# Linear attention into a gated feed-forward layer, in fp32 split into two parts on one core: matmuls with a lower part last within each word of matmuls, and a new order of all words

## The chip, the core and the metric

The kernel runs on one core of a Trainium2 chip. The core has TensorE (PE: matmuls, and PEld: the loads of their stationary tiles), VectorE (DVE), ScalarE (ACT), GpSimd (POOL) and SyncE (SP, which issues the DMAs here). Each engine executes its own list of instructions in order and waits on semaphores for the others. The metric is the device time of one execution in microseconds (us).

## The reference

Attention with a decaying state over 32 batch-head pairs, 768 time steps and 48 columns, followed by a gated feed-forward layer over 3072 tokens:

```python
# q, k, v, alpha: (4, 8, 768, 48); w_gate, w_val: (384, 1536); w_out: (1536, 384)
for t in range(S):
    state = alpha[:, :, t, :, None] * state + einsum('bhd,bhe->bhde', k[:, :, t], v[:, :, t])
    y[:, :, t] = einsum('bhd,bhde->bhe', q[:, :, t], state)
x = y.transpose(0, 2, 1, 3).reshape(3072, 384)
g = x @ w_gate
silu = g * (1.0 / (1.0 + exp(-g)))
out = (silu * (x @ w_val)) @ w_out
```

The inputs of attention are float32; the three weight matrices arrive as float64, are read as pairs of 32-bit words and are cut to two float32 parts on the chip.

## The kernel before

**Precision.** Each operand of the large products is split into an upper part and a lower part, the rest that the upper part leaves (both in the format fp32r). A product of two operands is then three matmuls that add into the same PSUM tile: upper by upper, upper by lower, lower by upper. The fourth, lower by lower, is left out.

**Tiling.** The feed-forward layer takes 8 blocks of 384 tokens, and 12 slices of 128 of the hidden width for each, which are 96 steps (s = 0 to 95). Blocks 0 and 1 are each done in two parts (slices 0 to 6 of both, then 7 to 11 of both), with the partial sums of the output stored and read back between; the other blocks go one after the other. Attention is cut into 16 units of 192 time steps, in three chunks of 64; two units give the tokens of a block, so attention of later units runs between the products of earlier blocks.

**One step of the feed-forward layer** is made of these words:
- `g` and `v` (TensorE, `product`, L716): nine matmuls each into one PSUM tile (`gps` or `vps`, one buffer each): for each of three k-tiles (`kt`) the three matmuls above. The stationary operand is a weight tile (128x128), the moving one 128x384 of the turned x (`xT`).
- `sl` (ScalarE, L724): silu of g. `h` (VectorE, L728): its product with v. `hh` (ScalarE, L732): the upper part of h, `hl` (VectorE or GpSimd, L737): the lower part. h, hh and hl have two buffers each.
- `o` (TensorE, `out_product`, L748): nine matmuls, three for each of three PSUM tiles `ops0` to `ops2` (128 tokens each). The stationary operand is a tile of hh or hl, the moving one the upper or lower part of w_out. The sums stay in the ops tiles over the 12 steps of a block; `first` starts them and `last` closes them, and `ot` and `os` (or `pl`, the partial sums read back) take them out.

**One unit of attention** is made of loads (`La`, `Lk`, `Lq`, `V`), copies and transpositions into the layout of the scans (L397, L405 and L417), two scans of the decay over time (`G`, L461, and `f`, L470), products of k and q with their results (`mk`, L818 and L821; `q`), k turned back (`K`, L511, with its copies `kc` L515 and L516; or `kr`, L527, on VectorE), scores `S` (L552) and their mask `ma` (L586), the sums of k and v that are carried between chunks `B` or `Bw` (L576) with `ad` (L599 to L608) and `de`, a copy `vc` of V (`U`, L498), outputs `Y` (L630 to L647), their upper and lower parts `yh` and `yl` (L661, L665), and the repacking into x by DMA (`xr`, L701) or, for the first units, by TensorE (`R`, L687). Words `w0v0` to `w19p` cut the weights (L160 on ScalarE is one of their steps), and `wr`, `wc`, `Lc` and `ck` read inputs again to see whether they lie in the range that this path is made for; only if not, another path runs behind it.

**The order.** Nothing is scheduled by the compiler: the table `ORDER` is a list of words, each `engine:name@banks` with t for TensorE, v VectorE, s ScalarE, g GpSimd and y SyncE. A loop (L898 to L902) calls them in that order, and so fixes what each engine executes after what, which engine does a word that more than one can do, and which PSUM bank a tile takes (L895).

```python
BANKS = ("A0", "A1", "A2", "ops0", "ops1", "vps", "gps", "ops2")
...
for word in ORDER.split():
    e, name = word.split(":")
    name, *banks = name.split("@")
    todo.pop(name)(engines[e], *(BANKS[int(x)] for x in "".join(banks)))
```

## Time and profile before

| what | us |
|---|---|
| three runs | 552.26, 555.14, 554.64 |
| their median | 554.64 |
| the profiled execution, its own time | 552.74 |
| its span, from first to last instruction | 551.0 |

The profile is of one execution. A group in it is a set of instructions of one line, engine, operation and kind of tile: their count, busy time in us, the mean ns of one, and then the idle time of the engine just ahead of them with what ended it. TensorE's matmuls are pipelined, so one lasts longer (336 ns) than the time from one start to the next. In the chain of work that ended last a row is a start, a time and the work, with matmuls that follow each other closely in one row. A row of the stages has the stretch, its length, the busy time of TensorE's matmuls, of its weight loads, of VectorE, ScalarE and GpSimd with their counts of instructions, then the granted clock of TensorE, the share of the DMA engines and the GB/s that they moved. The chain of waits names for each group of an engine what released it: total us, count, longest.

### The profile page before, as it was taken

To read this page: it belongs to the slowest core of one execution; us is meant where nothing else is said; L and a number is where in the kernel's file an instruction comes from. 1 tells how busy PE (TensorE), PEld (TensorE's weight loads), DVE (VectorE), ACT (ScalarE), POOL (GpSimd) and SP (SyncE) were. 2 spreads that over 40 slices of the span, in tenths; PEclk is the share of its full clock that TensorE was granted. 3 is DMA by queue.
4 is the path that set the end of the run, shared out by engine and by line. 5 is a ranking of instruction groups with operands and counts; after the bars stand their busy time and mean duration, and the time that the engine had idled before them with its cause. 6 is when DMAs were issued, how large, how long until landed. Compare 5 with 4: busy or idle time off the path is not lost.

```text
span 551.0 us, 13702 instructions
## 1 busy us (share of the span) xinstructions
PE 536.4 (97%) x5510; PEld 523.7 (95%) x5510; DVE 384.8 (70%) x612; ACT 258.7 (47%) x581; POOL 136.5 (25%) x146
## 2 busy tenths in 40 slices
PE   4999999999999999999999999999999999999996
PEld 3899999999999989999999999999999999999996
DVE  7999999999999996766788378878765232321223
ACT  6998655353422232243332434235343345447775
POOL 7522124354314240122220322231230101001100
PEclk9999999999999999999999999999999999999999
DMA  8789859435668555343536526535351112334463
GB/s 254 193 246 292 249 145 251 130 95 133 164 170 223 134 130 152 82 119 79 119 100 184 158 56 178 135 87 165 82 159 47 47 49 82 104 106 131 123 181 100
DMA packets 95362, 77.61 MB, mean 141 GB/s; under 512 B 32832, under 2 KB 92224, under 8 KB 95296
## 3 DMA queue, kind: packets, MB, share of 16 engines
q1 hardware_dynamic: 94864, 76.12, 51.2%
q8 instruction: 44, 0.72, 0.6%
q10 hardware_dynamic: 432, 0.59, 0.3%
q14 instruction: 22, 0.18, 0.1%
HBM read 62.52 MB, written 5.90 MB: 124 GB/s over the span
## 4 chain that ended last, share of the span: by engine, by line
PE 90%; DVE 3%; SPq 2%; ACT 2%; DMA 1%; issue 1%; DVEq 0%; ACTq 0%
PE g L716 26%; PE v L716 26%; PE ops L748 26%; PE A L576 3%; PE y L647 2%; PE s L552 2%; PE y L630 1%; SPq L701 1%; PE y L631 1%; DVE AT L470 1%; PE pt L417 1%; PE kps L511 1%; DMA Le<-in_alpha_dram 1%; DMA L<-in_k_dram 1%; DVE Gs L461 1%
## 5 line engine op out<-in xcount | busy, mean ns | idle before, releaser
L716 PE MATMUL g<-xT,w 128*128 128x384 f32 x864 | 167.5, 337 | 1.0 <-issue 1.0
L716 PE MATMUL v<-xT,w 128*128 128x384 f32 x864 | 166.9, 337 | 0.3 <-DVE h L728 0.3
L748 PE MATMUL ops<-w,hh 128*128 128x384 f32 x576 | 157.4, 336 | 0.0
L716 PEld LDWEIGHTS g<-xT,w 128*128 128x128 f32 x864 | 151.0, 188 | 2.2 <-issue 1.3
L716 PEld LDWEIGHTS v<-xT,w 128*128 128x128 f32 x864 | 150.9, 188 | 1.4 <-DVE h L728 0.9
L737 POOL TENSOR_TENSOR hl<-h,hh 128x384 fp32r<-128x384 f32 x63 | 67.7, 1076 | 308.1 <-ACT hh L732 294.1
L728 DVE TENSOR_TENSOR h<-h,v 128x384 f32<-128x384 f32 x96 | 53.1, 553 | 102.2 <-PE v L716 98.3
L732 ACT CAST hh<-h 128x384 fp32r<-128x384 f32 x96 | 49.0, 513 | 141.4 <-DVE h L728 74.4
L748 PEld LDWEIGHTS ops<-w,hh 128*128 128x128 f32 x576 | 105.3, 188 | 0.2
L748 PE MATMUL ops<-w,hl 128*128 128x384 f32 x288 | 96.7, 336 | 0.0
L724 ACT ACTIVATE h<-g 128x384 f32<-128x384 f32 x96 | 47.0, 490 | 77.7 <-PE g L716 68.6
L527 DVE STREAM_TRANSPOSE K<-Gs 32x384 f32<-32x384 f32 x96 | 54.7, 570 | 1.9
L748 PEld LDWEIGHTS ops<-w,hl 128*128 128x128 f32 x288 | 54.1, 188 | 0.0
L737 DVE TENSOR_TENSOR hl<-h,hh 128x384 fp32r<-128x384 f32 x33 | 18.8, 576 | 22.6 <-ACT hh L732 22.4
L470 DVE TENSOR_TENSOR_SCAN AT<-AT,back 128x771 f32<-128x771 f32 x16 | 32.5, 2031 | 0.6
L586 DVE TENSOR_TENSOR X<-s,mask 64x384 f32<-64x384 f32 (+1 forms) x48 | 26.1, 552 | 5.3 <-PE s L552 2.5
L461 DVE TENSOR_TENSOR_SCAN Gs<-AT,inj 128x772 f32<-128x772 f32 x16 | 28.9, 1804 | 1.1 <-ACT AT L794 0.9
L661 ACT CAST X<-y 112x384 fp32r<-112x384 f32 x28 | 12.5, 478 | 32.3 <-PE y L647 32.3
L665 DVE TENSOR_TENSOR X<-y,X 112x384 fp32r<-112x384 f32 x28 | 15.2, 552 | 14.0 <-ACT X L661 13.8
L318 ACT ACTIVATE wc<-wc,wbias 128x384 f32<-128x384 f32 x36 | 23.3, 647 | 1.2
L576 PE MATMUL A<-V,K 64*48 64x48 f32 (+1 forms) x720 | 21.5, 206 | 0.7 <-issue 0.7
L345 POOL TENSOR_TENSOR w<-t,w 128x768 fp32r<-128x768 f32 (+1 forms) x9 | 15.7, 1746 | 22.7 <-ACT w L341 17.8
(118 smaller groups left out, 579.2 us busy)
## 6 DMA issues: line engine op xcount, KB each, us to landing
xT<-X SPq DMA_DIRECT2D x84, 72.0 KB, 2.2
raw<-in_moe_w_gate_dram SPq DMA_DIRECT2D x12, 384.0 KB, 4.7
raw<-in_moe_w_val_dram SPq DMA_DIRECT2D x12, 384.0 KB, 5.8
raw<-in_moe_w_out_dram SPq DMA_DIRECT2D x12, 384.0 KB, 5.5
V<-in_v_dram SPq DMA_DIRECT2D x96, 48.0 KB, 3.5
wc<-in_moe_w_gate_dram SPq DMA_DIRECT2D x12, 384.0 KB, 3.8
wc<-in_moe_w_out_dram SPq DMA_DIRECT2D x12, 384.0 KB, 3.4
wc<-in_moe_w_val_dram SPq DMA_DIRECT2D x12, 384.0 KB, 3.6
```

The costliest lines, as they stand in the source:

```text
L318: nc.scalar.activation(dev, dev, AF.Relu, bias=wbias, scale=-1.0, accum_out=wviol[:, 0, i : i + 1])
L461: nc.vector.tensor_tensor_scan(*(x.rearrange("p g t -> p (g t)")[:, ::-1] for x in (Gs, AT, inj)), 0.0, op0=ALU.mult, op1=ALU.add)
L470: nc.vector.tensor_tensor_scan(Af, Af, back[:, 1 : n + 1], back[:, 0:1], op0=ALU.mult, op1=ALU.add)
L527: nc.vector.transpose(out=bass.AP(k0.tensor, k0.offset, [k0.ap[0], (G * 2 * D, NU), (2 * D, G), (1, 32)]), in_=Kg[j * BO + x : j * BO + x ...
L576: nc.tensor.matmul(to[j * BO : j * BO + D, g - gs.start, :], Ks[r, x, g, KC[j]], Vd[r, x, g, VC[j]], start=(x == 0 or not whole), stop=(x ...
L586: nc.vector.tensor_tensor(out=X[r, z, f * GF : (f + 1) * GF, :].rearrange("r g (c t) -> r g c t", c=NU), in0=sps[f][r].rearrange("r g (c t ...
L716: nc.tensor.matmul(pt, wsp[kind, f][a][:, kt * P : (kt + 1) * P], xT[blk][:, b_, kt, :], start=(n == 0), stop=(n == 3 * KT - 1),)
L724: nc.scalar.activation(h, acc.pop(("g", blk, f)), AF.Silu)
L728: nc.vector.tensor_tensor(out=h, in0=h, in1=acc.pop(("v", blk, f)), op=ALU.mult)
L732: nc.scalar.copy(out=hh, in_=acc["h", blk, f])
L737: eng.tensor_tensor(out=hl, in0=acc.pop(("h", blk, f)), in1=hh.bitcast(F32), op=ALU.subtract)
L748: nc.tensor.matmul(ops[blk][i], h[b_][:, i * P : (i + 1) * P], wsp["o", f][a], start=(first and n == 0), stop=(last and n == 2),)
```

## The change

It has two parts. **Inside a word**, the matmuls change places. A product goes over the three k-tiles with the upper weight part by the upper and the lower part of x first, and then over the three with the lower weight part. An ops word goes over the three ops tiles with hh by the upper and the lower part of w_out, and then over the three with hl; the words that close the ops tiles (`last`) keep the three matmuls of a tile together. The matmuls themselves and their number stay.

```diff
-    HL = ((0, 0), (0, 1), (1, 0))
...
     def product(kind, blk, f):
         pt = acc[kind, blk, f] = ps.tile([P, NB], F32, tag=kind + "ps", name=f"{kind}{blk}_{f}")
         n = 0
-        for kt in range(KT):
-            for a, b_ in HL:
-                nc.tensor.matmul(
-                    pt, wsp[kind, f][a][:, kt * P : (kt + 1) * P], xT[blk][:, b_, kt, :],
-                    start=(n == 0), stop=(n == 3 * KT - 1),
-                )
-                n += 1
+        for kt, a, b_ in [(kt, 0, x) for kt in range(KT) for x in range(2)] + [(kt, 1, 0) for kt in range(KT)]:
+            nc.tensor.matmul(
+                pt, wsp[kind, f][a][:, kt * P : (kt + 1) * P], xT[blk][:, b_, kt, :],
+                start=(n == 0), stop=(n == 3 * KT - 1),
+            )
+            n += 1
...
         h = hT.pop((blk, f))
-        for i in range(NTT):
-            for n, (a, b_) in enumerate(HL):
-                nc.tensor.matmul(
-                    ops[blk][i], h[b_][:, i * P : (i + 1) * P], wsp["o", f][a],
-                    start=(first and n == 0), stop=(last and n == 2),
-                )
+        HL = ((0, 0), (1, 0), (0, 1))
+        todo_ = [(i, n) for i in range(NTT) for n in range(2)] + [(i, 2) for i in range(NTT)]
+        for i, n in sorted(todo_) if last else todo_:
+            a, b_ = HL[n]
+            nc.tensor.matmul(
+                ops[blk][i], h[b_][:, i * P : (i + 1) * P], wsp["o", f][a],
+                start=(first and n == 0), stop=(last and n == 2),
+            )
```

**The table ORDER** is another one, nearly all of its lines. Its words are the same but for the engine that some of them run on: VectorE takes three more of the `hl`, two more of the `mk` and five more of the `ot` words, and two fewer of the `q` words; GpSimd takes four `qc`, two `vc` and two `w..a` words from ScalarE. The line around step 60, for one:

```diff
-g:mk14 v:f14 t:g60 t:v60 s:sl60 v:h60 s:hh60 t:g61 s:sl61 y:V13.4 t:v61 t:o59 v:hl60 v:h61 s:hh61 g:vc12 t:Y12@65
...
+v:G14 v:f14 t:g60 s:sl60 y:wr32 t:v60 v:h60 t:o57 t:o58 s:hh59 g:hl59 v:tk14 g:mk14 v:kr13.2 v:kr13.0 t:g61 s:sl61
```

What this does on the engines is seen best where the instructions stand. A row is a line of the kernel, the operation, the tiles (out<-in) and the size, with a count where the same stands several times in a row; each kernel has its own numbers in the names of tiles. In the change the lines of the products are L714 instead of L716, of the ops words L748, of silu, h, hh and hl L722, L726, L730 and L735.

TensorE at the first ops word (step 0: ops_0 to ops_2 are its PSUM tiles, hh and hl the parts of h, w the two parts of the weights in one tile), before:

```order
L716 MATMUL v_2_1057<-xT_529,w_666 128x384 x9
L748 MATMUL ops_0_0_1069<-w_676,hh_0_784 128x384
L748 MATMUL ops_0_0_1069<-w_676,hl_0_786 128x384
L748 MATMUL ops_0_0_1069<-w_676,hh_0_784 128x384
L748 MATMUL ops_1_0_1070<-w_676,hh_0_784 128x384
L748 MATMUL ops_1_0_1070<-w_676,hl_0_786 128x384
L748 MATMUL ops_1_0_1070<-w_676,hh_0_784 128x384
```

and in the change:

```order
L714 MATMUL v_2_1028<-xT_526,w_677 128x384 x9
L748 MATMUL ops_0_0_1042<-w_674,hh_0_778 128x384 x2
L748 MATMUL ops_1_0_1043<-w_674,hh_0_778 128x384 x2
L748 MATMUL ops_2_0_1044<-w_674,hh_0_778 128x384 x2
L748 MATMUL ops_0_0_1042<-w_674,hl_0_780 128x384
L748 MATMUL ops_1_0_1043<-w_674,hl_0_780 128x384
L748 MATMUL ops_2_0_1044<-w_674,hl_0_780 128x384
```

The pair of hh by the upper and the lower weight part is one row of x2 now, and the hl matmuls of all three tiles stand behind the hh ones.

ScalarE in the opening, from the copies SE and V of unit 0's carried sums (from the PSUM tiles s and A) to the copies of unit 1's k (from kps); t is a step of the cut of a weight, U the copy of V. Before:

```order
L606 COPY SE<-s_0_234 48x96 x2
L606 COPY SE<-A_0_295 48x96 x2
L599 COPY V_77<-A_0_295 48x8x48 x2
L160 ACTIVATE t_352<-raw_350,lbias 128x384
L498 COPY U<-V_77 64x3x96 x2
L515 COPY K_105<-kps_2_357 64x4x48
L516 COPY K_105<-kps_2_357 64x4x48
L515 COPY K_105<-kps_1_370 64x4x48
L516 COPY K_105<-kps_1_370 64x4x48
```

and in the change:

```order
L606 COPY SE<-s_0_235 48x96 x2
L606 COPY SE<-A_0_292 48x96 x2
L515 COPY K_105<-kps_2_350 64x4x48
L516 COPY K_105<-kps_2_350 64x4x48
L160 ACTIVATE t_357<-raw_345,lbias 128x384
L599 COPY V_77<-A_0_292 48x8x48 x2
L498 COPY U<-V_77 64x3x96 x2
L515 COPY K_105<-kps_1_373 64x4x48
L516 COPY K_105<-kps_1_373 64x4x48
```

The two copies from kps_2 and the cut t stand ahead of V now, and only V's copy U stays right behind it.

VectorE around step 60 (h_0 is its h, h_11 that of step 59; Gs and AT are the tiles of the scans of unit 14, whose L461 and L470 these rows call SCALAR_TENSOR_TENSOR and the trace TENSOR_TENSOR_SCAN; trk is its k turned). Before:

```order
L728 TENSOR_TENSOR h_10_4779<-h_10_4779,v_10_4769 128x384
L397 STREAM_TRANSPOSE AT<-L_72 128x4x6x32
L527 STREAM_TRANSPOSE K_105<-Gs_4534 32x12x32 x2
L461 SCALAR_TENSOR_TENSOR Gs_4812<-AT,inj 128x772
L728 TENSOR_TENSOR h_11_4814<-h_11_4814,v_11_4816 128x384
L397 STREAM_TRANSPOSE trk_4840<-L_71 128x4x6x32
L467 RECIPROCAL back<-Gs_4812 128x4
L470 SCALAR_TENSOR_TENSOR AT<-AT,back 128x771
L471 MEMSET AT 128x3
L728 TENSOR_TENSOR h_0_4870<-h_0_4870,v_0_4860 128x384
```

and in the change:

```order
L397 STREAM_TRANSPOSE AT<-L_72 128x4x6x32
L726 TENSOR_TENSOR h_11_4810<-h_11_4810,v_11_4812 128x384
L586 TENSOR_TENSOR X_103<-s_12_4686,mask 128x384
L461 SCALAR_TENSOR_TENSOR Gs_4824<-AT,inj 128x772
L467 RECIPROCAL back<-Gs_4824 128x4
L470 SCALAR_TENSOR_TENSOR AT<-AT,back 128x771
L471 MEMSET AT 128x3
L726 TENSOR_TENSOR h_0_4839<-h_0_4839,v_0_4843 128x384
L397 STREAM_TRANSPOSE trk_4876<-L_71 128x4x6x32
```

The transposition of k into trk, which stood ahead of the scan L470 and of step 60's h, stands behind both.

More of the change, by code (lines that the diff above doesn't have):

```diff
@@ L139 @@
[L139 to L141 removed]
+y:La0 y:wl0 v:w0v0 v:w0v1 v:w0v2 s:pa0 t:Ta0@12 s:ea0 v:G0 y:Lq0 s:pq0 y:La1 s:pa1 t:Ta1@63 y:wl1 s:w1v0 s:w0a g:w0p
+v:f0 t:Tq0@40 v:q0 y:Lk0 s:pk0 t:Tk0@15 v:mk0 v:w1v1 y:Lk1 s:pk1 s:ea1 v:G1 v:w1v2 y:Lq1 y:wl3 y:V0.0 t:Tk1@40 s:ek1
@@ new lines @@
+s:hh60 v:hl60 v:yl12.1 v:yl12.0 y:V14.4 t:S13@12 t:B13@0 v:ma13.1 v:ma13.0 t:g62 s:sl62 s:wc5 v:ot59.2 t:v62 v:ot59.1
+t:o60 t:o61 v:h62 s:hh62 g:hl62 v:de13 v:ad13.0 v:kr14.1 v:kr14.2 t:g63 s:sl63 t:v63 v:h63 v:kr14.0 s:hh63 v:ad13.1
+v:ad13.2 y:wr21 s:wc21 t:g64 t:v64 y:La15 t:o62 s:sl64 v:h64 v:ma13.2 g:vc13 t:Y13@15 s:yh13.0 g:hl63 v:kr14.3
+y:os59.2 y:os59.1 y:xr12.0 y:xr12.2 y:xr12.1 g:q14 y:V14.3 t:S14@26 v:ma14.2 y:V14.5 t:B14@0 s:yh13.1 v:yl13.1 t:g65
+t:v65 v:yl13.0 s:sl65 v:h65 s:hh64 g:hl64 y:wr16 s:wc16 v:tr15 v:de14 v:ad14.0 y:V15.5 t:g66 s:sl66 t:o63 t:o64 t:g67
@@ L142 @@
+v:ot95.1 y:Lc13 s:ck13 s:ot95.0 s:os95.0 s:os95.1 v:ot95.2 s:os95.2
 """
```

186 lines of the change are left out of this document (89 added, 97 removed).

## Prediction

> **What bounds the kernel now.** I read the page first, for the share of each engine and the chain that ended last; then the groups of TensorE; then the waits of TensorE alone, from the first product at 34 us to the last matmul at 546 us; then the places that these waits name.
>
> ```profile
> span 551.0 us, 13702 instructions
> ...
> PE 536.4 (97%) x5510; PEld 523.7 (95%) x5510; DVE 384.8 (70%) x612; ACT 258.7 (47%) x581; POOL 136.5 (25%) x146
> ...
> PE 90%; DVE 3%; SPq 2%; ACT 2%; DMA 1%; issue 1%; DVEq 0%; ACTq 0%
> ...
> L716 PE MATMUL g<-xT,w 128*128 128x384 f32 x864 | 167.5, 337 | 1.0 <-issue 1.0
> L716 PE MATMUL v<-xT,w 128*128 128x384 f32 x864 | 166.9, 337 | 0.3 <-DVE h L728 0.3
> L748 PE MATMUL ops<-w,hh 128*128 128x384 f32 x576 | 157.4, 336 | 0.0
> L748 PE MATMUL ops<-w,hl 128*128 128x384 f32 x288 | 96.7, 336 | 0.0
> ```
>
> TensorE is 97% busy, at a granted clock of 1.00 (the seventh number of the stage rows further down), and the chain that ended last is 90% TensorE. The last number of a group is the idle time ahead of it: the 288 matmuls that read the lower part of h (hl) follow with 0.0 us of it, and the 1728 of the products wait 1.3 us in all. A busy TensorE is not yet a TensorE at its best, so next comes how closely the words follow each other. This is the chain late in the run; each row is start, time, and a word of nine matmuls (x18 and x27 are two and three words):
>
> ```profile
> 41.54 1.59 PE g L716 x9
> ...
> 483.52 1.59 PE v L716 x9
> 485.11 4.70 PE ops L748 x27
> ...
> 491.38 1.56 PE v L716 x9
> ...
> 499.30 1.59 PE g L716 x9
> 500.89 3.14 PE ops L748 x18
> ...
> 513.39 4.69 PE ops L748 x27
> ```
>
> A word takes 1.56 us (491.38), 173 ns a matmul, in most of the run; three ops words together take 4.69 or 4.70. There are 192 + 96 = 288 words, so 288 x 1.56 = 449 us of the span are words at that step. In some stretches a word takes 1.59 us; 40 of the single words of the chain stand at 1.58 to 1.60 us, the first at 41.54 us and the last at 499.30 us. The last two such stretches end at ops words (485.11, 500.89).
>
> What TensorE waits for from 34 to 546 us is three rows, and the weight loads show the same place again:
>
> ```profile
> PE g L716 <- issue: 1.0, 1, 1.0
> PE A L576 <- issue: 0.7, 1, 0.7
> PE v L716 <- DVE h L728: 0.3, 1, 0.3
> PEld v L716 <- DVE h L728: 0.9, 2, 0.7
> ```
>
> So 2.0 us of 512 are waits, and only 0.3 us of them (0.7 us at the weight load) are for data. The rest of what a new order could save lies before 34 us:
>
> ```profile
> 0.00:35.00 35.00, 27.13 (x539) 23.57 (x540) 30.55 (x51) 29.14 (x66) 21.76 (x39) 1.00 0.82 228
> PE pt L417 <- POOL sel L369: 5.1, 1, 5.1
> PE pt L417 <- ACT wide L405: 1.5, 2, 1.3
> ```
>
> TensorE (the first engine of the row) is idle for 35.00 - 27.13 = 7.9 us there, 5.1 us of it ahead of its first matmul, which stands behind set-up that the list of words doesn't order.
>
> **The change, part by part.** Counts first: both lists have the same 366 words for TensorE, 21 stretches of attention words between products in both, and neither adds nor drops a matmul. So the 449 us of words stay, and what can change is the step inside a word, waits, and what feeds them.
>
> *Lower parts last, in products and ops words.* A wait for hl now falls on the seventh matmul of nine instead of the second, one for the lower weights of a product on the seventh instead of the third: 4 or 5 steps of 173 ns, 0.7 to 0.9 us of grace (an ops word reads its lower weights one matmul earlier, at its second). But the waits it would shorten aren't there: idle 0.0 us ahead of the hl group, none for weights among TensorE's waits from 34 us on. Gain 0. As for the step, products now stay on one PSUM tile with each upper weight twice in a row, as before, while ops words change tile every third matmul and the stationary operand every matmul; both take 1.56 to 1.57 us. So neither changing tiles nor repeating a stationary operand has a visible price, and the new mixture should keep the step: term 0. Bounds: -40 x 0.03 = -1.2 us, if every slow word becomes fast, and (288 - 40) x 0.03 = +7.4 us, if all become slow.
>
> "TensorE: Matmul & The Clock Gate" of the Trainium skill (Part 2, LDWEIGHTS) says that weights can be loaded once and used for many matmuls, and its section on the back-to-back gap gives N/2.4 + 2.5 ns, 162.5 ns for 384 columns. By that the 288 ops matmuls that now repeat their stationary tile could save 10.5 ns each, an estimate of 3.0 us; the trace, with pairs in the products and none in the ops words at one step of 173 ns, gives 0.
>
> *The opening.* ScalarE's order changes around the copy of V that the first y word needs:
>
> ```profile
> 18.77 0.49 ACT L606 COPY SE<-A 48x96 f32<-48x96 f32 x2
> 19.28 0.97 ACT L599 COPY V<-A 48x384 f32<-48x384 f32 x2
> 20.28 0.65 ACT L160 ACTIVATE t<-raw,lbias 128x384 f32<-128x384 uint32 x1
> 20.95 0.89 ACT L498 COPY U<-V 64x288 f32<-64x288 f32 x2
> 21.86 0.31 ACT L515 COPY K<-kps 64x192 f32<-64x192 f32 x1
> 21.89 0.33 PE L647 MATMUL y<-X,U 64*64 64x64 f32 x8
> 22.83 0.31 ACT L516 COPY K<-kps 64x192 f32<-64x192 f32 x1
> 23.20 0.92 PE L552 MATMUL s<-X,Gs 48*64 48x64 f32 x44 [0.29 <-ACT K L516]
> ```
>
> Now two of the copies of K (about 0.65 us) and the L160 cut (0.67 us with its step) go ahead of V. V starts at 19.28 + 1.32 = 20.60 and ends at 21.57, U ends at 20.60 + 0.97 + 0.9 = 22.47 instead of 21.84: the first y word, which starts its U matmuls at 21.89 now, does so 0.6 us later. What is late next is S1: today it has its first matmuls out by 22.6 and then stands until 23.20 for the copy that ends at 23.14. In the new list S1 uses the bank whose K copy has moved forward, so that wait goes. -0.6 + 0.6: near nothing. I take +0.1, with -0.5 and +0.7 as bounds (the wait goes and y isn't late; y is late and the wait stays).
>
> *The one wait for h, at 366 us.*
>
> ```profile
> 360.39 1.65 DVE L397 STREAM_TRANSPOSE trk<-L 128x768 f32<-128x768 f32 x1
> 362.09 3.34 DVE L470 TENSOR_TENSOR_SCAN AT<-AT,back 128x771 f32<-128x771 f32 x1
> 365.54 0.56 DVE L728 TENSOR_TENSOR h<-h,v 128x384 f32<-128x384 f32 x1
> 362.11 1.70 POOL L821 TENSOR_TENSOR Gs<-trk,Gs 128x768 f32<-128x768 f32 x1
> L470 DVE TENSOR_TENSOR_SCAN AT<-AT,back 128x771 f32<-128x771 f32 x16 | 32.5, 2031 | 0.6
> ```
>
> h60 stands behind a transposition and a scan, and this scan takes 3.34 us against a mean of 2.03, with GpSimd's 1.70 us product running beside it. The new list puts the scan and h60 ahead of the transposition, and that product can only start behind the transposition; and TensorE gets o57, o58 and g61 (three words, 4.7 us) between v60 and the v61 that waits for h60, where it had one word. The wait goes: -0.5 us, between the 0.3 idle on TensorE and the 0.7 at the weight load. It could also appear elsewhere, as 16 such scans remain: bounds -0.7 and +0.5.
>
> *The two waits for nothing ("issue").*
>
> ```profile
> 202.95 0.44 PE L716 MATMUL g<-xT,w 128*128 128x384 f32 x1
> 204.40 0.44 PE L716 MATMUL g<-xT,w 128*128 128x384 f32 x1 [1.01 <-issue]
> 391.22 0.24 PE L576 MATMUL A<-V,K 64*48 64x48 f32 x2 [0.74 <-issue]
> q8 instruction: 44, 0.72, 0.6%
> ```
>
> One falls on the second matmul behind the stretch Y7 S8 B8, the other inside B14 of Y13 S14 B14. Attention words are where TensorE issues most instructions in a microsecond, and instructions come by 44 packets of 0.72 MB / 44 = 16 KB, so I read these as TensorE waiting for its own program. In the new list both stretches have as many matmuls ahead of them as before, and g30 behind the first. I expect both again: 0, with -(1.28 + 0.9) = -2.2 us if both go (1.28 is the 1.45 us from matmul to matmul at 204.40 less a step) and +1.7 us, as much idle time again, if two more stretches meet one.
>
> *Work moved between engines.* VectorE gets three more of the hl subtractions, two more of the k products and five more output copies, and loses two q products. From 35 to 200 us it is nearly full:
>
> ```profile
> 35.00:115.00 80.00, 80.00 (x840) 78.15 (x842) 75.95 (x101) 49.85 (x92) 22.17 (x20) 1.00 0.72 203
> 115.00:200.00 85.00, 85.00 (x988) 83.21 (x982) 80.24 (x134) 29.50 (x64) 31.92 (x28) 1.00 0.62 161
> ```
>
> VectorE (the third engine) leaves 165 - 156.2 = 8.8 us idle there, and TensorE waited for none of it. Two words at least (3.1 us) stand between a v word and its ops word in both lists, so I cost this at 0. If the cover is gone, one place costs what the wait for h cost, 0.5 us.
>
> **Sum.** 0 + 0.1 - 0.5 + 0 + 0 = -0.4 us. The profiled execution took 552.74 us (1.7 us around its span), so 552.3 on its clock. The three runs of before are 552.26, 555.14 and 554.64; the profiled one is 1.9 us under their median and their mean is 554.0. Against that mean: **553.6 us**.
>
> **Rivals.**
> - *Faster, the stalls go together.* The waits for h and issue, the slow words and the opening's bound: -0.7 - 2.2 - 1.2 - 0.5 = -4.6 us, 549.4. For it: the list moved everywhere, and each of these depends on exact places. Against: the two issue places have the same work ahead. Half of it is still "no change". Chance 0.22.
> - *Slower, the slow step spreads.* In the chain above the 1.59 us stretches end at ops words, which alternate hh and hl; the new ones go hh, hh three times, then hl three times. If these no longer end a slow stretch, it runs on to the next attention words. It decides from 2.8 / 0.03 = 93 more slow words; half of the 248 fast words would cost 3.7 us: 557.3. Against: products don't alternate and stand at 1.56 as well. Chance 0.10.
> - *Slower, VectorE is late between 35 and 200 us*, six times 0.5 us: 556.6. For it: 8.8 us of slack in 165. Against: no such wait there now and hardly more work in that stage. Chance 0.06.
> - *A repeated stationary tile is cheaper.* Products with pairs and ops words without differ by 0.01 us a word: 96 x 0.01 = 1 us, 552.6. The skill's rule above would make it 3.0. Chance 0.04, and still "no change".
>
> **Chances and range.** 0.5% of 554 is 2.8 us, about what a measurement of this kernel can tell from no change. My forecast, with its own bounds mostly inside that, has 0.58, and the repeated tile 0.04: no change 0.62. Faster 0.22, slower 0.16. The range goes to the faster rival at 549.4 and to the pitch rival at 557.3, and leaves out the far ends: 549.5 to 557.5.
>
> **What would show it.** Right: groups of products and ops at 336 to 337 ns with idle time near 0, nine matmuls in 1.56 us, TensorE's waits from 34 us on below 3 us in all, no wait for h at v61, issue waits again near B14 and g30, the first g word within 1 us of 34.5 us. Wrong: chain rows of 1.59 us behind ops words (the slow step), a PE row waiting for DVE h or hl in 35 to 200 us, issue rows that are gone or twice as many, or a first product word that is 2 us off.

## The result, and the profile after

The changed kernel takes **558.22 us** (median of 14 runs, 554.95 to 563.81), the one before on the same chip **553.93 us** (median of 14, 552.26 to 556.37): a ratio of **1.0062 (interval 1.0040 to 1.0083)**. Ratios here and below leave out slow runs (one of these 14, three of the 11 of `front_after`, two of the 6 of `opening_before_store_early`) while the medians hold all runs, so a ratio is not the quotient of two medians. The change is slower; whether by more than the bound of 0.5% the interval leaves open. The median lies 0.7 us above the predicted range. The profiled execution took 557.15 us, 555.4 us of it span.

From the page of the changed kernel: span, engines, chain that ended last, and the groups of the words.

```profile
span 555.4 us, 13696 instructions
...
PE 538.1 (97%) x5510; PEld 526.3 (95%) x5510; DVE 385.7 (69%) x620; ACT 250.9 (45%) x564; POOL 143.2 (26%) x155
...
PE 93%; DMA 3%; issue 1%; SPq 1%; DVE 1%; ACT 0%; POOL 0%; DVEq 0%; ACTq 0%
...
L714 PE MATMUL v<-xT,w 128*128 128x384 f32 x864 | 166.9, 337 | 0.0
L714 PE MATMUL g<-xT,w 128*128 128x384 f32 x864 | 166.8, 337 | 0.0
...
L748 PE MATMUL ops<-w,hh 128*128 128x384 f32 x576 | 121.0, 339 | 1.8 <-DVE part L756 1.5
...
L748 PE MATMUL ops<-w,hl 128*128 128x384 f32 x288 | 69.3, 337 | 0.0
```

The products no longer wait for anything, and hl is as punctual as it was. New is one wait of 1.5 us of the ops words for `part`, the partial sums that are read back (ot, L756). The smaller busy time of the ops groups is no gain: the same tiles stand next to each other now, and the overlap of their matmuls is counted once. The chain shows the real step of a word:

```profile
113.20 3.13 PE ops L748 x18
...
127.81 1.56 PE v L714 x9
```

Two ops words in 3.13 us, a product in 1.56: the pitch did not change. What TensorE waited for from 34 us on (chain of waits: total us, times, longest):

```profile
PE A L576 <- issue: 1.6, 3, 0.8
PE ops L748 <- DVE part L756: 1.5, 1, 1.5
PE ops L748 <- DVE X L665: 0.3, 1, 0.3
```

The stages, in the columns of the prediction's stage rows:

```profile
0.00:35.00 35.00, 25.18 (x524) 22.67 (x525) 29.04 (x47) 27.46 (x61) 20.54 (x40) 1.00 0.76 218
...
115.00:200.00 85.00, 82.76 (x974) 80.58 (x973) 76.91 (x129) 26.14 (x55) 29.62 (x25) 0.98 0.56 144
200.00:555.40 355.40, 350.20 (x3211) 344.77 (x3209) 204.58 (x347) 147.75 (x356) 66.69 (x69) 1.00 0.43 115
```

Idle time of TensorE before 35 us is 9.8 us (before: 7.9), from 115 to 200 us 2.2 us (before: 0.0), behind 200 us 5.2 us (before 351.0 - 344.3 = 6.7, with the wait for h60 and one of the two issue waits). So +1.9 + 2.2 - 1.5 = +2.7 us more idle (with rounding), and 1.7 us more busy, about 1.6 of them from 3.41 us at half clock near 165 us (the 0.98 of that stage): together the 4.4 us between the spans.

The order of the words gives the same picture by another way: lateness of the k-th word of nine matmuls against before's profiled run, in us.

| kernel (profiled run) | 3rd | 7th | 25th | 61st | 73rd | 97th | 193rd | 288th |
|---|---|---|---|---|---|---|---|---|
| the change | 1.9 | 1.9 | 1.9 | 1.9 | 5.6 | 5.1 | 5.1 | 5.0 |

The first word, a g word at 37.05 us instead of 34.47, is 2.6 us late, the third 1.9. Another 3.7 us come at one place near step 19; the rest of the run gives 0.6 us back. Before's profiled run (552.74 us) is one of its faster ones, 1.2 us under their median, so lateness against a typical run of before is smaller by about that. The table of the experiments below uses the same measure.

### The profile page after: what moved, and what is told of

Its sections match the earlier page's. It is cut to its first block, busy times and chain, and to the rows that moved or that the text cites. A ratio compares the mean times of both kernels' runs of the same rounds, so it can differ in the third digit from the quotient of the medians.

```text
span 555.4 us, 13696 instructions
## 1 busy us (share of the span) xinstructions
PE 538.1 (97%) x5510; PEld 526.3 (95%) x5510; DVE 385.7 (69%) x620; ACT 250.9 (45%) x564; POOL 143.2 (26%) x155
## 4 chain that ended last, share of the span: by engine, by line
PE 93%; DMA 3%; issue 1%; SPq 1%; DVE 1%; ACT 0%; POOL 0%; DVEq 0%; ACTq 0%
PE ops L748 27%; PE g L714 27%; PE v L714 27%; PE A L576 3%; PE y L647 2%; PE s L552 2%; PE pt L417 1%; PE y L630 1%; PE y L631 1%; DMA Le<-in_alpha_dram 1%; DMA part<-scratch 1%; DMA out_dram<-part 1%; DMA V<-in_v_dram 1%; PE s L576 0%; PE xp L687 0%
## 5 line engine op out<-in xcount | busy, mean ns | idle before, releaser
L714 PE MATMUL v<-xT,w 128*128 128x384 f32 x864 | 166.9, 337 | 0.0
L714 PE MATMUL g<-xT,w 128*128 128x384 f32 x864 | 166.8, 337 | 0.0
L714 PEld LDWEIGHTS v<-xT,w 128*128 128x128 f32 x864 | 150.9, 188 | 0.9 <-DVE h L726 0.3
L714 PEld LDWEIGHTS g<-xT,w 128*128 128x128 f32 x864 | 150.8, 188 | 0.6
L735 POOL TENSOR_TENSOR hl<-h,hh 128x384 fp32r<-128x384 f32 x60 | 67.3, 1122 | 308.2 <-ACT hh L730 297.7
L726 DVE TENSOR_TENSOR h<-h,v 128x384 f32<-128x384 f32 x96 | 53.0, 553 | 103.9 <-PE v L714 85.8
L748 PE MATMUL ops<-w,hh 128*128 128x384 f32 x576 | 121.0, 339 | 1.8 <-DVE part L756 1.5
L748 PEld LDWEIGHTS ops<-w,hh 128*128 128x128 f32 x576 | 102.9, 189 | 2.6 <-DVE part L756 1.8
L730 ACT CAST hh<-h 128x384 fp32r<-128x384 f32 x96 | 49.1, 512 | 122.0 <-DVE h L726 96.1
L722 ACT ACTIVATE h<-g 128x384 f32<-128x384 f32 x96 | 46.9, 488 | 102.1 <-PE g L714 98.6
L748 PE MATMUL ops<-w,hl 128*128 128x384 f32 x288 | 69.3, 337 | 0.0
L748 PEld LDWEIGHTS ops<-w,hl 128*128 128x128 f32 x288 | 52.3, 190 | 0.0
L470 DVE TENSOR_TENSOR_SCAN AT<-AT,back 128x771 f32<-128x771 f32 x16 | 30.7, 1917 | 0.6
L461 DVE TENSOR_TENSOR_SCAN Gs<-AT,inj 128x772 f32<-128x772 f32 x16 | 28.4, 1776 | 1.1 <-ACT AT L794 0.6
L735 DVE TENSOR_TENSOR hl<-h,hh 128x384 fp32r<-128x384 f32 x36 | 19.9, 555 | 12.5 <-ACT hh L730 11.3
L345 POOL TENSOR_TENSOR w<-t,w 128x768 fp32r<-128x768 f32 (+1 forms) x10 | 20.2, 2029 | 13.0 <-DVE X L586 5.6
```

The source lines that it names most:

```text
L461: nc.vector.tensor_tensor_scan(*(x.rearrange("p g t -> p (g t)")[:, ::-1] for x in (Gs, AT, inj)), 0.0, op0=ALU.mult, op1=ALU.add)
L470: nc.vector.tensor_tensor_scan(Af, Af, back[:, 1 : n + 1], back[:, 0:1], op0=ALU.mult, op1=ALU.add)
L714: nc.tensor.matmul(pt, wsp[kind, f][a][:, kt * P : (kt + 1) * P], xT[blk][:, b_, kt, :], start=(n == 0), stop=(n == 3 * KT - 1),)
L722: nc.scalar.activation(h, acc.pop(("g", blk, f)), AF.Silu)
L726: nc.vector.tensor_tensor(out=h, in0=h, in1=acc.pop(("v", blk, f)), op=ALU.mult)
L730: nc.scalar.copy(out=hh, in_=acc["h", blk, f])
```

## The experiments

**Theories.** (W) The new order inside a word costs time. (L) TensorE waits for its own instructions at more places. (R) The read-back of the partial sums at step 19 is late because SyncE issues a store late, and half clock follows. (P) GpSimd's lower part of h is late. (O) The opening is what counts. Kernels are named `a_` for the change with something undone, `b_` for before with something added, `front_` for a table that is before's up to a point. AFTER and BEFORE are the two tables. Each ratio is against before on the same chip.

| kernel | us (median) | ratio, interval |
|---|---|---|
| a_again (the change, another chip) | 561.50 | 1.0116 (1.0081 to 1.0151) |
| b_new_word_order | 557.43 | 1.0033 (1.0012 to 1.0054) |
| b_new_word_again | 558.26 | 1.0048 (1.0032 to 1.0063) |
| a_old_word_order | 562.61 | 1.0121 (1.0077 to 1.0164) |
| a_store_early | 559.75 | 1.0079 (1.0048 to 1.0110) |
| b_reload_late | 556.96 | 1.0030 (1.0007 to 1.0052) |
| a_shift | 565.26 | 1.0157 (1.0119 to 1.0194) |
| a_shift_store_early | 562.88 | 1.0141 (1.0105 to 1.0176) |
| b_shift | 558.43 | 1.0056 (1.0038 to 1.0073) |
| b_shift_later | 557.05 | 1.0029 (1.0009 to 1.0050) |
| front_before | 554.54 | 0.9978 (0.9959 to 0.9996) |
| front_before_old_words | 554.58 | 0.9978 (0.9965 to 0.9992) |
| front_after | 564.79 | 1.0116 (1.0082 to 1.0151) |
| opening_before_store_early | 564.61 | 1.0115 (1.0062 to 1.0168) |
| a_hl1_vector | 561.99 | 1.0091 (1.0061 to 1.0122) |
| a_hl1_vector_store_early | 561.83 | 1.0090 (1.0066 to 1.0114) |
| front_before_65us | 556.94 | 1.0020 (0.9993 to 1.0047) |
| front_before_65us_store_early | 556.73 | 1.0026 (1.0004 to 1.0048) |

### The order inside a word, alone (W)

`b_new_word_order` and `b_new_word_again` are before's table with the new loops of product and out_product; `a_old_word_order` is the new table with the old loops.

```diff
-        for kt in range(KT):
-            for a, b_ in HL:
+        for kt, a, b_ in [(kt, 0, x) for kt in range(KT) for x in range(2)] + [(kt, 1, 0) for kt in range(KT)]:
```

> The kernel before with the new order of matmuls inside product and ops words, and its own table of words. Theory 1: within 0.2% of before (553 to 555 us), words at 1.56 us. Theory 2 (the order inside words is what makes it slower): 557 to 558 us. The rival of the prediction that a repeated stationary tile is cheaper: 551 to 553 us.

> The kernel before with the new order inside words once more, on this chip. If that order costs by itself: 0.3% above before again. If the first measurement was the chip's state: within 0.2%.

> The change with the old order of matmuls inside product and ops words, and its new table. Theory 1: within 1 us of the change (557 to 559 us), unless the ops words that now have hl in second place wait for it: each such word shows as a wait for hl on TensorE. Theory 2: 553 to 555 us.

Undoing the loops in the new table gains nothing (1.0121 beside 1.0116 for the change on another chip). The words keep their step: where two follow each other, a product takes 1.56 us and an ops word 1.57 (medians) in each of the twenty traces. Alone in before's table the new loops make the span, from first to last instruction, 1.1 us shorter (median 552.3 against 553.4 on that chip) and 1.0 us shorter in the second set of runs (552.7 against 553.7); some 0.6 us of that lies behind the last word (4.3 us to the end in the traces with the new loops, 4.8 to 5.0 with the old ones). Yet the time is 0.3 to 0.5% longer, because these two kernels spend 4.5 to 5.9 us around their span in all 22 runs, where every other kernel of the study spends 1.7 to 1.9. Their traces show what is there: five packets of the two instruction queues (q8 and q14) start 2.8 to 3.8 us behind the last instruction and end 5.0 us behind it, where in every other trace the last such packet starts ahead of the last instruction. So the likely reason is a late load of the program's end, and not the order of the matmuls; no run moved that load alone. `front_before` and `front_before_old_words`, further down, have both orders with one table and are equal. The term of 0 holds, and the rival of a slow step falls.

### The late read-back (R)

SyncE issues the store os18.2 in the new table at 152.62 us (timeline of SP: start, time, queue), and the load that brings the partial sums of the last tile stands behind it and behind work that reuses its buffer:

```profile
152.62 0.45 SPq L765 DMA_DIRECT2D out_dram<-part  x1
...
156.72 0.35 SPq L770 DMA_DIRECT2D part<-scratch  x1
```

In before the same two rows of SP are:

```profile
149.15 0.38 SPq L765 DMA_DIRECT2D out_dram<-part  x1
...
152.29 0.35 SPq L770 DMA_DIRECT2D part<-scratch  x1
```

The store is 3.5 us late, 1.9 of them from the opening; the load behind it 4.4 us.

VectorE's ot18.0 needs that load, and o19 needs ot18.0 to free its PSUM tile. One row of the change's timeline of VectorE (start, time, instruction, and in brackets the idle time ahead of it with its releaser):

```profile
161.04 0.56 DVE L756 TENSOR_TENSOR part<-ops,part 128x384 f32<-128x384 f32 x1 [3.40 <-DMA part<-scratch]
```

And its timeline of TensorE there:

```profile
158.31 1.83 PE L714 MATMUL v<-xT,w 128*128 128x384 f32 x9
161.65 0.62 PE L748 MATMUL ops<-w,hh 128*128 128x384 f32 x2 [1.51 <-DVE part L756]
162.58 1.14 PE L748 MATMUL ops<-w,hh 128*128 128x384 f32 x4 [0.31 <-DVE X L665]
163.51 1.16 PE L748 MATMUL ops<-w,hl 128*128 128x384 f32 x3
164.47 2.12 PE L748 MATMUL ops<-w,hh 128*128 128x384 f32 x6
```

VectorE stood 3.40 us for the load, TensorE 1.51 + 0.31 us behind it. Then nine matmuls that should start over 9 x 0.173 = 1.56 us (161.65 to 163.21) reach to 164.47, less 0.31 of wait: half clock for some of them. The clock that the trace records is 0.50 from 163.19 to 166.60 us and 1.00 around it. The stage row of this place shows it in the column behind the five engines:

```profile
158.00:170.00 12.00, 10.18 (x61) 9.49 (x56) 8.79 (x14) 1.89 (x4) 1.01 (x1) 0.86 0.36 91
```

`a_store_early` moves the store ahead; `b_reload_late` delays the load in before's table.

```diff
 a_store_early
-... y:xr4.2 g:q6 s:sl21 g:qc6 y:wr8 v:ad5.1 v:ad5.2 y:os18.2 t:v21
+... y:os18.2 y:xr4.2 g:q6 s:sl21 g:qc6 y:wr8 v:ad5.1 v:ad5.2 t:v21
 b_reload_late
-... y:Lk7 y:pl18.0 y:wr19 ... y:V7.0 y:V7.2
+... y:Lk7 y:wr19 ... y:V7.0 y:V7.2 y:pl18.0
```

> The change with one SyncE word moved: the store of the partial sums of block 0, rows 2 (os18.2), stands ahead of the repack xr4.2 and the range load wr8 instead of behind them. Theory 1 (the wait of step 19's ops word for the partial sums read back, and the lower clock behind it, make most of the loss): the store goes out some 1.5 to 1.8 us earlier, the read back pl18.0 with it, the 1.67 us wait of the ops word is gone or below 0.4 us, TensorE's matmuls behind it stay at 173 to 178 ns instead of 320, the granted clock is 1.00 over the span, and the time is 3 to 4 us below that of the change: 554 to 555.5 us. Theory 2 (the order inside a word costs steps, and the wait is only where it shows): the wait goes and the time falls by less than 1.5 us. Theory 3 (instruction loads make the loss): 557 to 558.

> The kernel before with one SyncE word moved the other way: the read back of partial sums pl18.0 stands behind two loads of V (V7.0, V7.2) and the range load wr19 instead of ahead of them, some 2.7 us later by the trace of before. Theory 1: step 19's ops word waits 1 to 2.5 us for it, the matmuls behind it run at about 320 ns for 2 to 4 us, the granted clock falls to 0.995 to 0.998 over the span, and the time is 2.5 to 5 us above before. Theory 2 and 3: a wait of that size alone, 1 to 2 us above before, and no matmuls at 320 ns.

In `a_store_early` the load is issued at 156.10 and the wait is 0.2 instead of 1.5, with no half clock behind it (waits of that kernel from 155 to 170 us):

```profile
PE ops L748 <- DVE X L665: 0.3, 1, 0.3
PE ops L748 <- DVE part L756: 0.2, 1, 0.2
```

So the mechanism is shown. Its size in the time is not: 1.0079 (1.0048 to 1.0110) is no better than the change. `b_reload_late` makes the wait in before's table (0.5 us, without half clock behind it) and costs 0.30% (0.07 to 0.52), 0.8 us of lateness at that place. Three more pairs with and without the early store follow below: 1.0157 and 1.0141, 1.0091 and 1.0090, 1.0020 and 1.0026, each pair within its intervals. In the traces the early store does save time at this place (0.7 to 1.3 us of lateness between words 61 and 73 in four of them, 2.0 to 4.1 us in six with the late store); why no median shows it stays open. Step 19 is 3.7 us of the one profiled execution, and not shown to set the median.

### Where the instructions come from (L)

The trace names no releaser for "issue". But it holds the 44 packets of the instruction queue, 16 KB each, and beside every issue wait one of these has just ended:

| kernel | TensorE goes on at | packet of 16 KB | end of packet to going on |
|---|---|---|---|
| before | 204.40 | 201.90 to 202.94 | 1.46 |
| before | 391.22 | 388.63 to 389.74 | 1.48 |
| the change | 25.81 | 23.28 to 24.18 | 1.63 |
| the change | 30.90 | 28.32 to 29.26 | 1.64 |
| the change | 396.40 | 393.92 to 394.79 | 1.61 |
| a_hl1_vector | 56.32 | 53.63 to 54.89 | 1.43 |
| b_shift | 162.38 | 159.74 to 160.98 | 1.40 |

In all traces these times lie between 1.25 and 1.65 us. A second count agrees: numbered along TensorE's list of instructions as the traces hold it, all 78 issue waits of the twenty traces fall on instruction 193 or 194 of a stretch of 256, and 16 KB in 256 instructions are 64 bytes for each. The waits come where TensorE reaches a boundary of these blocks soon after the one before, 2.9 to 5.1 us in the change, which happens in the stretches of attention words. To move the boundaries, `a_shift`, `a_shift_store_early` and `b_shift` add 26, 26 and 24 small matmuls (4 instructions of TensorE each) early in the opening, `b_shift_later` 24 at v22. They write into a PSUM tile that the real work then overwrites, so they change nothing but the count and the time that they take.

```diff
+            for _ in range(26 if (u, i, hf) == (1, 0, 0) else 0):
+                nc.tensor.matmul(pt[0:C, 0, 0:C], ident[0:D, 0:C], ident[0:D, 0:C], start=True, stop=True)
```

> The change with 26 more small matmuls (104 TensorE instructions) ahead of unit 1's first transposition, where TensorE waits for the copy of alpha anyway; nothing else moves. Theory 3 (issue waits are TensorE waiting for the next 256 of its instructions, and they come where two such loads fall into one stretch of attention words): the loads fall 104 instructions earlier in the words, one each to Y6, Y12 and Y13 and the next behind B7, B13 and B14, so the three issue waits there (0.61, 0.57 and 0.94 us in the trace of the change) are gone, those of the opening stay, and the time is 2 to 4 us below that of the change on this chip. The rival (these waits belong to the words, for a reason the profile doesn't show): the same words wait as before, and the time is within 1 us of the change or up to 1 us above it.

> The shift and the earlier store of partial sums together. If the wait for the partial sums with its low clock and the issue waits are separate losses: 4 to 6 us below the change, at or below before, and the granted clock at 0.997 or more in every run. If the store alone gains nothing (as its own run beside before hinted), no lower than the shift alone.

> The kernel before with 24 more small matmuls (96 TensorE instructions) at the same place. Theory 3: its issue waits behind Y7 S8 B8 and inside B14 (1.28 and 0.93 us in its trace) are gone, and it is 1.5 to 3 us faster than before. The rival: they stay, and it is within 0.5 us of before or slower.

> The kernel before with 24 small matmuls (96 TensorE instructions) ahead of step 22's v word, behind Y5 S6 B6, instead of in the opening: they cost about 0.6 us there. Theory 3 (two loads of instructions in one stretch of attention words make TensorE wait): no issue waits in Y6 to B14 (2.2 us in the trace of before), the opening as before, so 1 to 2 us faster than before or the same where its own runs had none; more important, a narrower spread. The rival (the waits come with the words): 0.6 us slower than before.

The waits moved with the boundaries: those at the old places went, and a new, longer one came in the stretch Y5 S6 B6, where two boundaries fall now. The waits of `b_shift`, then of `a_shift`:

```profile
PE s L578 <- issue: 2.2, 1, 2.2
```

```profile
PE ops L750 <- POOL hl L737: 3.2, 1, 3.2
PE s L578 <- issue: 2.5, 1, 2.5
```

That an issue wait is a late block of instructions is thus shown by moving it. What such a wait is worth these four kernels can't show, because the added matmuls cost more than they were meant to. The trace holds two for each (48 for 24). Their rows in the chain, of `b_shift` and then of `b_shift_later` with the v word behind them, are:

```profile
6.63 5.31 PE pt L417 x48
```

```profile
158.33 2.16 PE v L714 x37
161.68 2.91 PE v L718 x9
```

In `b_shift` they stand on the chain of work for 5.31 us, and the first g word starts at 38.13 us (34.47 in before). In `b_shift_later` all 48 take about 2.9 us, and the v word behind them runs at half clock, 2.91 us instead of 1.56. Behind the last word both have 7.5 us to the end instead of 4.8. So the 1.0029 of `b_shift_later`, with 0.5 us of issue waits left from 34 us on against 1.7, is a gain and a larger cost in one number.

From 34 us on the change's profiled run has 2.1 us of these waits and before's 2.2 (with what the word after the wait loses), as the prediction's term has it. In the opening the change has 0.92 and 0.56 us, where before's trace has none and the prediction didn't look. But these two come with before's opening as well (0.78 and 0.56 us in `b_new_word_order`, 1.03 and 0.28 in `front_before_65us_store_early`). Over whole traces, TensorE's idle time at these waits adds up to 1.5 to 2.9 us in the four with before's table and no added matmuls (mean 2.2), and to 3.1 to 6.0 us in the six with the change's table (mean 4.7; some kernels of both groups have a word moved or the other loops). So the new table has some 2.5 us more of them, as a mean of single executions; the profiled runs of before and the change alone show 1.3 us more.

### Where the loss lies (O): tables of two halves

```diff
 front_before
-ORDER = AFTER
+ORDER = BEFORE up to t:g24, then the words of AFTER that are left, in AFTER's order
 front_before_65us
+ORDER = BEFORE up to t:g4, then AFTER
 opening_before_store_early
+ORDER = BEFORE up to t:v1, then AFTER, with os18.2 early
 front_after
+ORDER = AFTER up to t:g24, then BEFORE
```

`front_before_65us_store_early` has the early store as well, `front_before_old_words` the old loops inside words.

> The new order inside words, with the table of before up to the first product of step 24 (some 175 us) and the table of the change for all words that are left. Theory 1 (the loss sits in the opening, in the wait of step 19 for partial sums and the low clock behind it; the rest of the new table costs little): the first g word stands before 36.2 us, no wait of step 19, and 0 to 0.4% above before (at most 1.5 us more for issue waits in Y7 to B14). The rival (the new order inside words, or the new table's later part, makes the loss): 0.6% or more above before.

> The same cut the other way: the table of the change up to the first product of step 24, then the table of before, with the new order inside words. Theory 1: the first g word stands at 36.5 to 37.5 us, step 19 waits 1.5 us or more with matmuls at 320 ns behind it, and nearly the whole loss is there: 0.6 to 1.2% above before. The rival: 0 to 0.4%.

> The change with the table of before up to step 1's v word (some 46 us) and with the early store of partial sums. If the opening and the partial sums are the two causes: within 0.4% of before, and 2.5 us or more below the change. If the store is no cause, the wait at step 19 is smaller but the time stays 0.6% or more above before.

> The table of before up to step 24, then the table of the change, with the old order inside words. If the new order inside words only gives room for a late hl: slower than the same table with the new order (which was 0.2% faster than before) by what its ops words now wait for hl in second place, which its trace shows; if it changes nothing: 0.2% faster than before, too.

> The new order inside words, the table of before up to the first product of step 4 (some 65 us), then the table of the change with its late store at step 18. If the loss lies before 65 us and at step 19: TensorE's words stand as in before up to step 18, step 19 waits about 1.6 us with matmuls at 320 ns behind it, and the time is 0.4 to 0.8% above before. If the loss is spread over the new table: 0.9% or more.

> The same with the early store of partial sums. If these two places are the loss: within 0.25% of before, 2 us or more below the run beside it. If it is spread: 0.5% or more above before.

With before's order up to step 24 the new table is as fast as before and a little faster: 0.9978 (0.9959 to 0.9996), and the same with the old loops. With the new order only up to step 24 it is slow: 1.0116. With before's order up to 65 us it is at 1.0020 (0.9993 to 1.0047). Taking before's order only up to about 46 us (`opening_before_store_early`) doesn't help: 1.0115. So the new order behind step 24 costs nothing. How the loss ahead of it divides depends on which of the change's two ratios is taken, for all these stand on different chips: with the 1.0116 of the second set of runs, 0.96 of 1.38% lie ahead of 65 us and 0.42 between there and step 24; with the 1.0062 of the first, 0.42 lie in each.

| kernel (profiled run), us late | 3rd | 7th | 25th | 61st | 73rd | 97th | 193rd | 288th |
|---|---|---|---|---|---|---|---|---|
| front_before | 0.2 | 0.2 | 0.3 | 0.3 | 0.8 | 0.9 | 2.0 | 2.3 |
| front_before_65us_store_early | 1.7 | 1.7 | 2.2 | 2.2 | 3.0 | 3.5 | 4.6 | 4.6 |
| a_again | 2.0 | 3.4 | 7.4 | 7.4 | 9.4 | 12.4 | 12.1 | 12.8 |
| a_hl1_vector | 3.1 | 6.9 | 6.9 | 7.0 | 10.7 | 10.7 | 11.2 | 11.3 |
| opening_before_store_early | 1.1 | 1.1 | 8.3 | 9.0 | 10.2 | 10.7 | 10.8 | 11.4 |

Between the 3rd and the 25th word one of two things goes wrong in the last three. The first is an instruction block that comes late. In the second chunk of attention there (Y2), the packet that TensorE needs next starts at 46.55 us in before, 49.11 in the change, 51.28 in `a_again` and 53.63 in `a_hl1_vector`. That is 0.8, 1.5, 3.6 and 4.9 us after TensorE crosses the block boundary ahead of it, and TensorE waits 0, 0, 1.19 and 2.23 us for it. In the ten traces that have before's order and its block boundaries up to there, the packet starts at most 1.9 us after the crossing and TensorE never waits; in the seven with the change's order it starts 1.5 to 5.0 us after, and TensorE waits in four. The stages 40 to 46 and 46 to 65 us of before, and then of `a_hl1_vector` (the last two columns are the DMA share and GB/s; a transfer counts whole where it starts, so a share can pass 1):

```profile
40.00:46.00 6.00, 6.00 (x120) 5.75 (x119) 5.51 (x10) 4.88 (x11) 1.66 (x3) 1.00 0.94 292
46.00:65.00 19.00, 19.00 (x324) 17.95 (x321) 18.06 (x29) 14.54 (x29) 3.38 (x3) 1.00 0.96 276
```

```profile
40.00:46.00 6.00, 6.00 (x80) 5.75 (x78) 5.43 (x8) 4.96 (x11) 0.19 (x1) 1.00 0.77 190
46.00:65.00 19.00, 16.77 (x321) 15.60 (x319) 16.83 (x26) 13.52 (x28) 3.31 (x4) 0.91 1.07 277
```

Before fills the DMA engines evenly (0.94, 0.96); in the new table SyncE issues the weight loads so that they stand at 0.77 and are then overfilled (1.07), and the instruction packet is among that traffic. That the overfill is what delays the packet is an inference from the times: no run changed the loads alone. The change's own profiled run has 0.68 and 1.07 there and no wait; so this cause strikes in some executions of the new order and not in all.

### The lower part of h on GpSimd (P)

The second thing is hl of step 1. In `opening_before_store_early` GpSimd takes 7.93 us for it where it takes 1.02 in before and 1.03 in the change. The timeline of GpSimd in the change, then in `opening_before_store_early`:

```profile
57.88 1.03 POOL L735 TENSOR_TENSOR hl<-h,hh 128x384 fp32r<-128x384 f32 x1 [0.66 <-ACT t L160]
```

```profile
57.71 7.93 POOL L735 TENSOR_TENSOR hl<-h,hh 128x384 fp32r<-128x384 f32 x1 [1.67 <-issue]
```

Some rows of VectorE in that time:

```profile
58.16 0.94 DVE L161 SCALAR_TENSOR_TENSOR t<-raw,t 128x768 uint32<-128x768 uint32 x1
60.36 1.81 DVE L164 SCALAR_TENSOR_TENSOR t<-raw,t 128x768 uint32<-128x768 uint32 x2
63.83 0.94 DVE L164 SCALAR_TENSOR_TENSOR t<-raw,t 128x768 uint32<-128x768 uint32 x1
64.70 0.54 DVE L726 TENSOR_TENSOR h<-h,v 128x384 f32<-128x384 f32 x1
```

And TensorE:

```profile
60.13 1.22 PE L748 MATMUL ops<-w,hh 128*128 128x384 f32 x6
65.70 1.33 PE L748 MATMUL ops<-w,hl 128*128 128x384 f32 x3 [4.35 <-POOL hl L735]
```

While VectorE cuts weights, instruction after instruction with two operands from SBUF, GpSimd's subtraction doesn't end; it ends (57.71 + 7.93 = 65.64) 0.94 us after VectorE has started h, which reads a PSUM tile. TensorE waits 4.35 us, and the grace of four matmuls that the new order inside the word gives is of no use against that. The same happened in `a_shift` (the 3.2 us row above), `a_shift_store_early` and `front_after`: 6.7 to 7.9 us in the four. "SBUF — State Buffer" of the Trainium skill (Who interferes with whom) says that a VectorE instruction with two SBUF inputs and a GpSimd one that reads SBUF contend for a port that one of them holds alone; the rows agree, with a duration of 7.9 against 1.0 us beside a whole run of such instructions. It is a matter of half a microsecond: in the change's own run hl starts at 57.88 us and VectorE has h and a mask, which read PSUM tiles, until the cuts begin at 58.89; in `opening_before_store_early` it starts at 57.71 us, and the cuts begin at 58.16.

`a_hl1_vector` gives this hl to VectorE, ahead of the cuts, with and without the early store:

```diff
-v:ma3.1 s:w7v0 v:w7v1 ... g:hl1 t:o1
+v:ma3.1 v:hl1 s:w7v0 v:w7v1 ... t:o1
```

> The change with the subtraction of step 1 (hl1) on VectorE, ahead of the cut of weight group 7, instead of on GpSimd. Theory 4 (GpSimd's hl1 gets no access while VectorE works back to back on two operands, so step 1's ops word waits 3 to 4.5 us in some runs, with a low clock behind it): no wait for hl near 65 to 69 us, no run above 562 us, the median 2 to 4 us below the change's 561.5 on the other chip, some 0.5% above before, since the wait of step 19 remains. The rival (hl1 is chance, the loss is the partial sums): 0.8% or more above before.

> Both: hl1 on VectorE and the early store of partial sums. If these two are the loss of the change: within 0.3% of before and the granted clock at 0.997 or more in most runs. If a third cause is left: 0.5% or more above before, with the wait still to be seen between 46 and 175 us.

Their traces have no wait for hl (nor had the two of the change itself), and the time isn't better: 1.0091 (1.0061 to 1.0122) and 1.0090 (1.0066 to 1.0114). Their profiled runs have 5.2 and 4.3 us of issue waits, and the second 1.5 us for an h. The first two rows of the waits of `a_hl1_vector`:

```profile
PE y L647 <- issue: 2.2, 1, 2.2
PE ops L748 <- DVE part L756: 1.5, 1, 1.5
```

### The change once more

> The change itself once more, as the yardstick on this chip beside the runs of before and of the three kernels below. Every theory: 0.4 to 1.0% slower than before, granted clocks between 0.99 and 1.00, and issue waits of TensorE in the stretches of attention words around Y6 B7, Y12 B13 and Y13 B14.

A second set of runs of the unchanged change on another chip gave 1.0116 (1.0081 to 1.0151), and its profiled run was 12.8 us late at the end. The first rows of its waits:

```profile
PE A L576 <- issue: 2.9, 2, 1.5
PE ops L748 <- DVE part L756: 1.4, 1, 1.4
PE g L714 <- DMA xT<-X: 1.3, 1, 1.3
PE y L647 <- issue: 1.2, 1, 1.2
```

They are the same kinds of waits as above, more of them, and one for a tile of x (`xT`) that no other wait here names, at a granted clock of 0.993 over the span. With 1.0062 on the first chip: the change is slower by 0.4 to 1.5%, in an amount that differs between the two sets of runs and from run to run.

## Why the prediction was wrong

**The steps that held.** *Pitch of the words, 0:* 1.56 us a product and 3.13 us two ops words. The rival of the slow step falls. So does that of the cheaper repeated tile, with 1 us as with 3.0: the words did not become quicker. *The wait for hl:* 0.0 us idle, as predicted. *Issue waits behind 34 us:* 2.1 against 2.2 us in the two profiled executions. That is partly luck: one of them came again near B14, the one at g30 did not, two others came, and over the traces the new table has more of them. The count of 21 stretches of attention words is 20 by the tables from the first product on, in both.

**The opening, +0.1.** The sum up to S1 came out nearly as worked out. The change's timeline of ScalarE:

```profile
20.74 0.96 ACT L599 COPY V<-A 48x384 f32<-48x384 f32 x2
21.72 0.89 ACT L498 COPY U<-V 64x288 f32<-64x288 f32 x2
```

V starts at 20.74 (20.60 worked out), U ends at 22.61 (22.47), the first y word's U matmuls start at 22.66 and S1 at 23.50 instead of 23.20: +0.3. But the third product word came 1.9 us late, and the difference is two instruction waits (the change's chain of work: start, time, what):

```profile
24.88 0.92 issue
25.81 0.79 PE A L576 x26
...
30.34 0.56 issue
30.90 0.68 PE y L647 x26
```

Against before's matmul steps at these places they cost 1.11 and 0.76 us. I bounded the term by the two ScalarE copies (-0.5 to +0.7) and did not count where blocks of instructions end; the issue row of the prediction was bounded for "two more stretches" at +1.7 us, and that is what came, in the stage that I had taken out of it. Not all of it is the order's: over the traces the third word is 1.1 to 3.1 us late with the change's opening (seven traces, mean 2.2) and 0 to 2.9 us with before's (ten, mean 1.2). So about 1 us of the 1.9 is the order, as a mean, and the rest these two executions.

**"I cost this at 0"** (work moved between engines) is the step that failed, with the opening beside it. Lateness of the words, one profiled execution against the other, is +1.9 us for the opening instead of +0.1 and +3.7 us at step 19 for a term of 0. The step argued from VectorE's slack between 35 and 200 us and from the distance of two words between v and ops. TensorE did not wait for a busy VectorE. It waited for a VectorE that waited 3.40 us for a load, which SyncE issued behind a store that the table had moved from 149.15 to 152.62 us. The step followed TensorE, ScalarE, VectorE and GpSimd and left out SyncE's queue, though the table moves its words too: stores and read-backs of the partial sums, and the weight loads. And it left out that a word on GpSimd (hl1) can take 7.9 us beside VectorE's cuts. Neither place is visible as a wait in before.

**The price of a wait.** The rival "VectorE is late" priced each wait at 0.5 us. The one measured is 1.51 + 0.31 us of wait and about 1.6 us of half clock on top (below), 3.7 us of lateness with what else the words there lose, where the rival's six places together came to 3.0.

**The wait for h at v61, -0.5.** It went there and came again at v60, which waits for h59: 0.16 us in the change, but 0.8 to 1.7 us in several others (from matmul to matmul, less a step). In the change's VectorE timeline h59 stands behind a transposition that waits for a load of alpha:

```profile
362.23 1.61 DVE L397 STREAM_TRANSPOSE AT<-L 128x768 f32<-128x768 f32 x1 [1.12 <-DMA L<-in_alpha_dram]
363.87 0.55 DVE L726 TENSOR_TENSOR h<-h,v 128x384 f32<-128x384 f32 x1
```

The prediction had looked at what the new order puts ahead of h60, and not at what it leaves ahead of h59.

**What is left open.** The halves of the table show that the loss lies ahead of step 24, and the profiled executions show what goes wrong there: instruction blocks in the opening and at Y2, hl1, the read-back at step 19, and half clock behind the longer waits. Which of them occurs in how many of the runs isn't shown. Each undone alone (early store, hl1 on VectorE) left the ratio within the intervals of the change's two sets of runs, and moving the block boundaries added costs of its own. So the mechanism that "I cost this at 0" missed is shown for one execution, and the shares of these causes in the 0.6 to 1.2% of the median are not settled; nor is the 0.2% (-0.07 to 0.47) that `front_before_65us` keeps.

## What to carry to other kernels

When a hand-made order is exchanged, follow every queue that the list orders, the one that issues the DMAs before all others: a store that moves a few words back delays a read-back, and the engine that shows idle slack is the one that then stands. Count the blocks of instructions (here 256 of TensorE's) through the stretches with the densest issue, and look what else the DMA engines carry there. An instruction that is added to move a boundary costs time of its own; read it from the trace before its median is read. An order that is even with the old one in its counts and slower in its median is best put back piece by piece: two runs with half a table each (0.9978 and 1.0116) said more than all the undone single words.

## What the hardware showed that I had not expected

- **Half clock after short waits.** The granted clock in the traces is 1.00 or 0.50, each fall to 0.50 ahead of the end lasts 3.41 us (6.83 us twice), and the times between falls are whole multiples of 3.41 us too. Cut into these stretches, all traces give one picture, from the first grant to 545 us: TensorE was idle for 1.59 us or more in 16 stretches at full clock, and all 16 are followed by one at half clock. With 1.45 to 1.49 us it is three of five, with 0.50 to 1.22 us none of 72. (One more fall, with 0.45 us idle, stands behind the added small matmuls of `b_shift_later`.) So two waits that fall into one stretch add up, as the 1.51 and 0.31 us of the change do, and a wait that the end of a stretch divides can go unpunished. The price is mostly ten matmuls at 320 ns from start to start instead of 174: 10 x 0.146 = 1.46 us. In the 14 runs of the change the time goes with the granted clock: 554.95 and 555.16 us at 0.998 and 1.000, 562.52 and 563.81 at 0.991 and 0.992, a correlation of -0.86. "TensorE: Matmul & The Clock Gate" of the Trainium skill (Part 1) describes a gate that looks at free-running windows of about 3.4 us. The 3.41 us here agree, but less than half a window of idle time was enough.
- **TensorE waits for its program.** Its blocks are 16 KB, a packet takes 0.9 to 2.5 us, and TensorE goes on 1.25 to 1.65 us after its end. The wait is up to 2.7 us (`a_old_word_order`) where two blocks end in one stretch of attention words, or where the packet starts late beside full DMA engines.
- **GpSimd can be kept out for 7.9 us** by a run of VectorE instructions that mostly last 0.94 us each.
- **4.5 to 5.9 us around the span** in all 22 runs of before's table with the new loops, where all other kernels have 1.7 to 1.9, with instruction packets that end 5.0 us behind the last instruction in both traces.
